# Duo attention and wave MLP on one core: V of the first batch in rows of six tokens, ordered by selecting matrices on TensorE; later V as one DMA a batch; filler products in the prologue; a new order of the steps on every engine

## The chip, the cores and the metric

One core of a Trainium2 chip. The metric is device microseconds of one execution (lower is better). All numbers with a point in time are microseconds from the start of the profiled span. The span in a profile is some 1.5 to 2 us shorter than the time. Engines: TensorE (PE in the profile, PEld its weight loads), VectorE (DVE), ScalarE (ACT), GpSimd (POOL), SyncE (SP). A run is called slow when it is over 1.5% above the fastest run of the same kernel; the others are called fast.

## The reference

Causal attention for 8 heads (three "retrieval" heads see everything before them, five "streaming" heads see 4 sink tokens and a window of 64), then an MLP that mixes tokens with a complex wave. B = 4, H = 8, S = 768, D = 64, d_model = 512.

```python
scores = q @ k.T / 8                       # per batch and head, 768 x 768
a = softmax(where(mask, scores, -1e9))
x = (a @ v) as [batch, 768, 512]
theta = x @ w_theta
zr, zi = x * cos(theta), x * sin(theta)
y = w_tok_r @ zr + w_tok_i @ zi            # over tokens
u = x + y
out = u + maximum(u @ w_ch, 0)
```

## The kernel before

The kernel describes its work as steps (engine, duration, what a step needs, which buffer it takes) and a small planner in the file orders them: list scheduling by the longest way to the end, plus a list `TILT` of corrections that was found by a search. The planner only fixes the order on each engine; on the chip each engine executes its own list in order and waits where something is missing.

```python
LATENCY = {"PE": (230, 0), "ACT": (190, 60), "DVE": (120, 60), ..., "DMA": (2000, 0), "DMAH": (2000, 0)}
rank[n] = longest way to the end + 100 * TILT[n]      # the highest rank that is ready goes first
...
def load_v(b, n, after=None):                # one pair of heads, rows of 64 f32 = 256 B
    src = v[b].rearrange("h (j p) d -> p h j d", p=128)
    ...
    for x, h in enumerate(PAIRS[n]):
        nc.sync.dma_start(out=t[:, x], in_=src[:, h])
def cast_v(b, n):                            # f32 -> bf16, DVE or GpSimd
    copy(vt[:, h0:h1 + 1:2, :, :D], state["v", b, n])
...
def v_steps(b):
    for n in range(4):
        if b == 0:
            issue = add("DVE", 200, lambda n=n: load_v(0, n, kT[n // 2]), [kept["k", 0, n // 2]], take="st_v")
            land = add("DMAH", 2000, None, [issue])
        else:
            issue = add("SP", 700, lambda b=b, n=n: load_v(b, n), [cast[b - 1, n], xk[b - 1, 5]], take="st_v")
            land = add("DMAH", 2000, None, [issue])
        cast[b, n] = add({"DVE": 570, "POOL": 830}, 0, lambda b=b, n=n: cast_v(b, n), [land] + old, give=[issue], port=True)
```

For each batch: 96 transposes of q and k, half-array scores (products that use half of the array's rows, some also half of its columns), exponentials on ACT, sink scores, value products (128x65), theta (24 products of 128x512), sines on ACT (another table than the exponential), z products on DVE, then 18 groups of four mix products and the channel products. Batch b+1's attention overlaps batch b's MLP. The value products need V with tokens on partitions; q, k (but for the first heads of batch 0) and the weights come by GpSimd's casting DMA.

The softmax here doesn't subtract the row's maximum and nothing guards it: scores larger than these inputs give would overflow.

## Time and profile before

| | before |
|---|---|
| time, median of the first 3 runs | 204.3 us (204.25 to 204.82) |
| span of the profiled run, mean granted clock | 201.1 us, 0.969 |
| TensorE, DVE, ACT busy | 88%, 64%, 52% |
| V of batch 0 landed | 23.45 |
| first theta product, last theta product | 34.38, 42.2 |
| TensorE idle before 50.63 | 3.96 us |

How to read it: TensorE is the busiest engine and from 60 us on it is nearly always busy, so the end is set by how much of TensorE's work is done by then. I use one derived number for that: *useful work by time t*, an estimate worked out from the traces. It counts the weight loads recorded until t (there is one for each product) and multiplies each by what a product of its shape takes at full clock in these traces (0.216 us for 512 columns, 31 ns for a value product, 56 or 28 ns for a transpose, 36 ns for a score, 56 ns for one of the few sink scores). Selecting and filling products are left out. The profile lines of the kernel before stand in the prediction.

Read the granted clock with care in the prologue. In the kernel before the column reads 1.00 until 25, while the starts of its products lie at half pace. The pace decides.

### The profile page before, as it was taken

The page shows a single profiled execution, that of the slowest core. Times are in us where ns is not written, and L with a number is a line of the kernel's source. Part 1 is how long each engine was busy: PE and PEld are TensorE (multiplying, and loading weights), DVE is VectorE, ACT ScalarE, POOL GpSimd, SP SyncE. Part 2 cuts the span into 40 slices and gives each one's busy share as a digit, 9 for nine tenths or more (in the row PEclk, how much of TensorE's full clock was granted, in tenths as well). Part 3 has the DMA queues.
Part 4 walks back from the last instruction along what each step waited for, and adds up shares of the span by engine and source line. Part 5 has one row for each costly group of instructions (what it writes and reads, how often), then busy time and mean ns, then how long its engine had stood idle before and what let it go on. Part 6 is the DMA issues. An engine that isn't in the chain of part 4 may idle for free.

```text
span 201.1 us, 4814 instructions
## 1 busy us (share of the span) xinstructions
PE 178.0 (88%) x1961; PEld 99.1 (49%) x1988; DVE 128.2 (64%) x229; ACT 104.6 (52%) x129; POOL 67.8 (34%) x141
## 2 busy tenths in 40 slices
PE   0689697992899998999899999999999999999981
PEld 0446496551444665645454565644434665444430
DVE  7336975892853785459965573698814776972461
ACT  2688814699167433388777605689774217700010
POOL 8987773542832360012284501024811100000000
PEclk9999969998599999999999999999999999999997
DMA  5998999999925199899149997579363564124512
GB/s 169 175 225 180 167 218 196 193 207 206 178 32 111 26 143 207 79 259 209 52 68 178 203 198 158 55 165 248 76 152 88 152 130 82 60 47 123 165 52 104
DMA packets 60652, 28.82 MB, mean 143 GB/s; under 512 B 44888, under 2 KB 57560, under 8 KB 60632
## 3 DMA queue, kind: packets, MB, share of 16 engines
q1 hardware_dynamic: 49816, 19.23, 45.7%
q0 software_dynamic: 10816, 9.31, 30.8%
q8 instruction: 15, 0.25, 0.5%
q14 instruction: 5, 0.04, 0.1%
HBM read 25.71 MB, written 6.29 MB: 159 GB/s over the span
## 4 chain that ended last, share of the span: by engine, by line
PE 71%; DMA 15%; ACT 5%; DVE 5%; issue 2%; SPq 0%; DVEq 0%; ACTq 0%
PE bank L555 28%; DMA st_v<-in_v_dram 10%; PE bank L578 9%; PE pair L419 9%; PE pair L532 8%; PE pair L506 8%; PE bank L353 6%; DMA xT<-x 3%; DMA uT<-u 3%; PE bank L598 2%; DVE zi L291 1%; ACT P_st L435 1%; PE bank L568 1%; ACT P L438 1%; DVE P_st L629 1%
## 5 line engine op out<-in xcount | busy, mean ns | idle before, releaser
L555 PE MATMUL bank<-zi,wtokTi 128*128 128x512 bf16 x139 | 39.0, 391 | 0.6 <-issue 0.5
L555 PE MATMUL bank<-zr,wtokTr 128*128 128x512 bf16 x134 | 37.2, 380 | 0.7 <-issue 0.2
L295 POOL TENSOR_SCALAR_AFFINE_SELECT P<-P 128x256 bf16<-128x256 bf16 (+1 forms) x48 | 18.4, 403 | 37.5 <-ACT P L438 19.0
L419 PE MATMUL pair<-qT,kT 64*64 64x128 bf16 (+6 forms) x380 | 26.2, 258 | 4.0 <-ACT P L438 1.5
L559 DVE TENSOR_TENSOR u<-x,bank 128x512 bf16<-128x512 bf16 x24 | 16.4, 687 | 15.9 <-PE bank L555 15.9
L438 ACT ACTIVATE P<-pair 128x1024 bf16<-128x1024 f32 (+2 forms) x24 | 21.5, 918 | 7.9 <-PE pair L419 7.8
L578 PE MATMUL bank<-w_ch_sb,uT 128*128 128x512 bf16 x89 | 23.3, 380 | 1.2 <-ACT uT L288 0.7
L532 PE MATMUL pair<-w_theta_sb,xT 128*128 128x512 bf16 x91 | 22.8, 379 | 1.1 <-DMA xT<-x 0.6
L419 PEld LDWEIGHTS <-kT 64*64 64x64 bf16 (+1 forms) x380 | 12.8, 109 | 20.4 <-issue 16.5
L555 PEld LDWEIGHTS <-wtokTi 128*128 128x128 bf16 x144 | 13.6, 100 | 17.0 <-issue 2.8
L582 DVE SCALAR_TENSOR_TENSOR ot<-bank,u 128x512 f32<-128x512 f32 x24 | 16.6, 690 | 8.2 <-PE bank L578 7.0
L291 DVE TENSOR_TENSOR zr<-x,ct 128x512 bf16<-128x512 bf16 x24 | 17.5, 760 | 3.4 <-ACT ct L537 3.0
L555 PEld LDWEIGHTS <-wtokTr 128*128 128x128 bf16 x144 | 12.4, 98 | 13.7 <-issue 1.3
L537 ACT ACTIVATE ct<-pair,half_pi 128x1024 f32<-128x1024 f32 x12 | 13.4, 1116 | 10.3 <-PE pair L532 7.1
L291 DVE TENSOR_TENSOR zi<-x,st 128x512 bf16<-128x512 bf16 x24 | 17.7, 758 | 0.0
L288 ACT COPY uT<-bank 128x512 bf16<-128x512 bf16 x5 | 2.9, 586 | 27.5 <-PE bank L568 27.5
L435 ACT ACTIVATE P_st<-pair 128x512 bf16<-128x512 f32 (+1 forms) x16 | 12.8, 812 | 8.5 <-PE pair L419 8.5
L513 DVE TENSOR_TENSOR x<-pair,r 128x512 bf16<-128x512 f32 x24 | 16.6, 692 | 0.8
L455 DVE TENSOR_TENSOR P_st<-P_st,m_stream 128x512 bf16<-128x512 bf16 (+2 forms) x24 | 12.0, 507 | 6.3 <-ACT P_st L435 5.2
L506 PE MATMUL pair<-vx,P_st 128*128 128x65 bf16 x120 | 15.5, 198 | 0.0
L506 PE MATMUL pair<-vt,P_st 128*128 128x65 bf16 x120 | 15.5, 198 | 0.0
L506 PE MATMUL pair<-vt,P 128*128 128x65 bf16 x252 | 14.9, 199 | 0.5 <-ACT P_st L435 0.5
(76 smaller groups left out, 270.0 us busy)
## 6 DMA issues: line engine op xcount, KB each, us to landing
st_v<-in_v_dram SPq DMA_DIRECT2D x32, 192.0 KB, 3.9
out_dram<-ot SPq DMA_DIRECT2D x24, 256.0 KB, 2.2
qb<-in_q_dram POOLq DMA_DIRECT2D x13, 192.0 KB, 6.0
kb<-in_k_dram POOLq DMA_DIRECT2D x13, 192.0 KB, 6.5
wtok<-in_moe_w_tok_r_dram POOLq DMA_DIRECT2D x3, 384.0 KB, 11.6
wtok<-in_moe_w_tok_i_dram POOLq DMA_DIRECT2D x3, 384.0 KB, 12.5
vx<-vt SPq DMA_DIRECT2D x3, 195.0 KB, 6.8
w_theta_sb<-in_moe_w_theta_dram POOLq DMA_DIRECT2D x1, 512.0 KB, 8.5
```

The source lines that it names most:

```text
L291: {"DVE": nc.vector, "POOL": nc.gpsimd}[state["step"].eng].tensor_tensor(o, a, b, ALU.mult)
L295: nc.gpsimd.affine_select(out=t, in_=t, compare_op=ALU.is_ge, fill=0.0, base=base, pattern=pattern, channel_multiplier=cm)
L419: nc.tensor.matmul(ps[half, yy, c:c + w], l, r, start=True, stop=True, skip_group_check=True)
L435: nc.scalar.activation(stream_out(banks[0][1], 2, q0, w), ps[:, :, :w].rearrange("p s (c x) -> p s c x", x=64), AF.Exp, scale=scale)
L438: nc.scalar.activation(P.rearrange("p (y c) -> p y c", y=2), ps[:, :, :w0], AF.Exp, scale=scale)
L506: nc.tensor.matmul(o, l, r, start=(m == 0), stop=True, skip_group_check=True)
L513: nc.vector.tensor_tensor(dst, av[:, :, :, :D], r.unsqueeze(3).to_broadcast([128, 2, 4, D]), ALU.mult)
L532: nc.tensor.matmul(ps[:, y], state["xT", b][:, kk, (i + y) * 128:(i + y + 1) * 128], w_theta_sb[:, kk], start=(kk == 0), stop=(kk == KD - 1))
L555: nc.tensor.matmul(py, wtokT[n][:, s, t * 128:(t + 1) * 128], z[:, s], start=(g == 0 and m == 0), stop=(g == 2 and m == 3))
L559: nc.vector.tensor_tensor(u, state["x", b][:, t], state.pop(("py", b, t)), ALU.add)
L578: nc.tensor.matmul(pc, uT[:, kk], w_ch_sb[:, kk], start=(kk == 0), stop=(kk == KD - 1))
L582: nc.vector.scalar_tensor_tensor(ot, state.pop(("pc", b, t)), 0.0, state.pop(("u", b, t)), ALU.max, ALU.add)
```

## The change

Intent: get V of batch 0 early and with large rows, so that the value products can start sooner; save DMA issues by loading the V of later batches in one piece; and keep TensorE's clock up in the prologue with small products.

- Batch 0: V comes by one casting DMA whose partition p holds tokens 6p to 6p+5 (1536 B rows). The order that the value products need is made on TensorE: six groups of six products with a 0/1 matrix `pick`, then ACT or DVE copies the sums to `vt`.
- Batches 1 to 3: one DMA for the whole V, four casts after it.
- 240 products `ident x ident` of 128 columns that the planner puts wherever TensorE would otherwise wait.
- The planner's model got a cold clock, contention between the two kinds of queues and a limit of DMAs in flight, the weight loads are no longer chained, and the list `TILT` was searched anew. So the order on every engine is another one.

```diff
+    def load_v0():
+        state["v0"] = t = v_room[:, 4:]...bitcast(BF16)...
+        nc.gpsimd.dma_start(out=t, in_=v[0].rearrange("h (p j) d -> p h (j d)", p=128))
+    def pick_v0(i):
+        pv = state["pv", i] = mine()
+        for j in range(NB):
+            c = 128 * i - j + NB - 1
+            nc.tensor.matmul(pv, pick[:, c:c + 128], state["v0"][:, :, j * D:(j + 1) * D], start=(j == 0), stop=(j == NB - 1))
+    def keep_v0(i):
+        copy(vt[:, :, i, :D], state.pop(("pv", i)).rearrange("p (h d) -> p h d", h=H))
...
-    def load_v(b, n, after=None):
...
-        for x, h in enumerate(PAIRS[n]):
-            nc.sync.dma_start(out=t[:, x], in_=src[:, h])
+    def load_v(b):
+        nc.sync.dma_start(out=v_room.rearrange("p h j d -> p (h j) d"), in_=v[b].rearrange("h (j p) d -> p (h j) d", p=128))
...
+    for n in range(240):
+        idle.append(add("PE", 56, lambda n=n: keep_busy(n), idle[-1:], ..., bias=-10 ** 9))
...
-    hold = [cast[0, 2]]
-    issue = add("POOL", 780, lambda: ...w_theta..., hold)
+    issue = add("POOL", 780, lambda: ...w_theta...)
...
 TILT = [ ... another list ... ]
(the rest of the planner's new model is cut)
```

## The prediction

> **What bounds the kernel now.** I read, in this order: the busy shares, the chain of waits that ended last, the busy times in stretches, TensorE's instructions in order of time, and the V tile's own view. The numbers in front are microseconds from the span's start.
>
> The busy shares first.
>
> ```profile
> PE 178.0 (88%) x1961; PEld 99.1 (49%) x1988; DVE 128.2 (64%) x229; ACT 104.6 (52%) x129; POOL 67.8 (34%) x141
> ```
>
> TensorE is the bound by share. Next: where do the missing 12% lie? The stretches say (columns: stretch, length, then busy time and count of TensorE, weight loads, DVE, ACT, POOL; granted clock, DMA share, GB/s):
>
> ```profile
> 15.00:20.00 5.00, 4.69 (x60) 3.10 (x58) 3.13 (x7) 4.24 (x7) 3.82 (x12) 1.00 0.92 184
> 20.00:25.00 5.00, 3.21 (x84) 2.48 (x80) 4.78 (x12) 4.50 (x7) 3.86 (x9) 1.00 0.96 163
> 25.00:30.00 5.00, 4.92 (x99) 4.61 (x96) 3.91 (x8) 0.65 (x2) 3.85 (x6) 0.66 1.18 218
> 45.00:50.00 5.00, 1.67 (x28) 0.94 (x25) 1.34 (x3) 4.83 (x6) 1.36 (x2) 0.89 1.21 211
> 50.00:60.00 10.00, 9.15 (x82) 4.50 (x86) 7.27 (x13) 3.56 (x6) 5.97 (x10) 0.72 0.57 105
> 60.00:70.00 10.00, 9.89 (x113) 5.34 (x107) 5.75 (x12) 5.66 (x8) 2.77 (x7) 1.00 0.33 67
> ```
>
> From 60 on TensorE is full (9.89 of 10), and stays at 98% or so. So only the first 56 us can be shortened by this change, and DMA is saturated there (share 0.92 to 1.21). The chain of waits shows what holds that stretch:
>
> ```profile
> 29.92 19.14 DMA st_v<-in_v_dram
> 49.06 0.03 issue
> ...
> 49.63 0.96 DVE kT L288
> ...
> 50.63 1.44 PE bank L598 x12
> ```
>
> The last V load of batch 1 takes 19.14 us from issue to landing; DVE waits in order behind its cast, and TensorE behind DVE (4.0 us idle). Then the instructions in order of time, for their pace:
>
> ```profile
> 9.71 0.85 PE L353 MATMUL bank<-ident,kb 128*64 128x128 bf16 x12
> 10.35 0.85 PE L353 MATMUL bank<-ident,qb 128*64 128x128 bf16 x12
> ...
> 25.16 0.25 PE L506 MATMUL pair<-vx,P_st 128*128 128x65 bf16 x1
> 25.21 0.25 PE L506 MATMUL pair<-vt,P_st 128*128 128x65 bf16 x1
> ...
> 29.25 0.19 PE L506 MATMUL pair<-vx,P_st 128*128 128x65 bf16 x1
> 29.28 0.19 PE L506 MATMUL pair<-vt,P_st 128*128 128x65 bf16 x1
> ...
> 38.15 0.53 PE L353 MATMUL bank<-ident,qb 128*64 128x128 bf16 x12
> 38.51 0.50 PE L353 MATMUL bank<-ident,kb 128*64 128x128 bf16 x12
> ```
>
> Look at starts, not durations. Twelve transposes take 0.64 us at 9.71 and 0.36 at 38.15; value products follow each other at 54 ns at 25 and at 30 ns at 29. TensorE runs at half speed from 5.2 to about 28.4, though the clock column says 1.00 until 25: the pace decides, the column has no record yet. After the 4 us gap it is slow again until about 56 (the 0.72 above).
>
> **What the Trainium skill says.** "TensorE: Matmul & The Clock Gate", What's actually happening: idle is 1.2 GHz, and about 3.4 us of sustained work gives 2.4 GHz. The trace agrees: dense value products from 24.5 to 28.4, 3.9 us, then twice the pace. The same page, Part 4: PE-mode transpose: transposes don't count as busy in the same way. The trace fits: TensorE was 4.69 of 5 us busy from 15 to 20, with half-array scores and transposes, and stayed slow. So the added full-array products should warm it. "DMA: Bandwidth & Descriptors", Specifications: at least 512 B per transfer for line rate, less is slow. V goes in 256 B pieces now, in 1536 B pieces (768 B after the cast) for batch 0 later. The trace gives 220 GB/s for V of batch 3 nearly alone (136 to 139), so 1.57 MB cost some 7 us of all engines; against it, q and k on the casting queue run at 145 to 184 GB/s of written bytes (5 to 8). Same page, SWDGE vs HWDGE vs iDMA: the cast in a DMA comes only from GpSimd; that is why batch 0's V moves to that queue.
>
> **The change part by part.**
> 1. V of batch 0: four f32 loads in 256 B rows and four DVE casts (0.56 us each) go; one casting load in 1536 B rows comes. It writes 0.79 MB, at some 165 GB/s 4.8 us instead of 7: 2 us of DMA less. It need no longer wait for K copies on DVE, so I expect it landed near 17 instead of 21.
> 2. Ordering V: 36 products of 128x512 by the selecting matrix. The theta products are the same shape, four in 0.86: 36 x 0.216 = 7.8 us of TensorE, plus six ACT copies of 128x512, 0.6 us each (ACT copies of uT take 0.586). In the changed order all 36 stand together in the middle of the scores, before sink scores and values: they are on the path.
> 3. 240 fillers of 128x128. Warm, 12 wtok transposes of that shape take 0.67 us from 33.48, 56 ns each: 13.4 us in all; the first 42 run at half speed, 2.4 us more. They stand where TensorE would wait, so mostly free; but they execute in order and also cost where it would not have waited.
> 4. Batch 1 to 3: V as one DMA of the same 256 B pieces. 24 issues of about 0.65 us on the queue's issuer become 3; the bytes cost the same, and no cast can start before all has landed.
> 5. A new order on every engine (read from the order of the built kernel's instructions, engine by engine): DVE now reaches V's casts only after eight of batch 0's twelve z products; more weight transposes come early.
>
> The sum, by equal work. Before reaches 56 having done: 96 transposes of q, k for batch 0 (8 x 0.34 = 2.7), scores 4, sinks 0.5, 148 value products (x 0.030 = 4.5), xT transposes 1.3, theta 24 x 0.216 = 5.2, batch 1's 96 transposes 2.7, 36 weight transposes 2.0, a few scores 0.6, 16 mix products 3.5: 27 us of warm work in 56.
>
> The changed order reaches its last filler having done 2.7 + 4 + 0.5 + 7.8 (selection) + 4.5 + 1.3 + 5.2 + two groups of batch 1 (0.7) + 48 weight transposes (2.7) = 29.4. With fillers 13.4 + 2.4 and a start at 1.4 (the identity is ready at 1.37) that is 46.6. To stand where before stood at 56 it lacks 27 + 7.8 - 29.4 = 5.4: 52.0. That is 4.0 us earlier if nothing else stalls.
>
> Against it I set stalls the fillers don't cover. GpSimd issues w_theta as number 38 of its queue, by its mask and memset durations near 21 (19.86 before). So DMA idles from 17 to 21, and what remains, 4.8 MB written by the casting queue and V's 1.57, takes 32 us at the 195 to 200 GB/s of before: until 53, no earlier than before. V, started after the selection near 27, competes and lands near 45 (before under contention: 1.57 MB at 4.4 us per 0.39 MB, 17.7 us); DVE gets there then. The last q, k of batch 1 land near 52 to 54, just when TensorE comes to them. I take 1.5 us for that, leaving 2.5. Fewer issues and a warm clock at 50 to 56 are partly in this already; for a better order in the full part (3.7 us of non-busy from 56 to 197) I give 0.8. Together 3.3: 204.3 - 3.3 = 201.0.
>
> **The rivals.**
> A. The fillers and selection eat the gain: the prologue was held by ACT and DMA, not by TensorE. For: ACT is busy 4.24 to 4.50 of 5 from 15 to 25, and gains 3.6 us of copies. Against: TensorE's half speed sits between ACT's steps in the chain. This makes 203 to 206.
> B. V of batch 1 lands later, as one piece behind the weights, and DVE stalls longer than before with all behind it. For: issue at 27 against 18, DMA full. Against: the bytes on the casting queue are spread and DVE's casts stand later. Landing at 50 instead of 45 would cost about 4: 204 or so.
> C. All of the hole at 46.7 to 50.6 and the slow stretch to 56 go, and loads come as they are needed: the full 4.0 plus 2 in the full part: 198.
>
> **The range.** The middle is 201.0; C and a milder A bound it: 197.8 to 204.4. Faster by 2% means under 200.2, slightly beyond the middle: 0.42. Within 2%: 0.53. Slower by 2% (over 208.4) needs B and A together: 0.05.
>
> **What would show it.** Right: value products of batch 0 at 30 ns from the first; 36 selecting products in about 8 us, ending near 27; no slow clock at 50 to 60; TensorE's idle before weight transposes (4.0) gone; last theta done near 43 to 46. V landing near 45 with DVE waiting under 2 us for it. Wrong: TensorE still slow among fillers; a wait of some us for weights before the values; a DVE wait of 4 us or more for V; waits for q, k loads at 46 to 54 of over 3 us; or idle time in the full part (TensorE under 97% busy from 60), where xT transposes may queue behind the single V load.

## The result

| | before | after |
|---|---|---|
| time, median of 4 runs of the same rounds | 204.28 us (203.52 to 204.82) | 207.42 us (206.90 to 207.69) |
| ratio, 95% interval | | 1.0154 (1.0115 to 1.0193) |
| span of the profiled run | 201.1 us | 205.2 us |

A ratio, here and below, compares the fast runs of one kernel with the fast runs of the kernel before from the same rounds. The us quoted beside it are medians of all runs, slow ones included, so the ratio of two medians is not quite the same. The change is 1.5% slower: within 2%, but above the range predicted (197.8 to 204.4).

The page of the changed kernel (its first part: busy time, share of the span, instructions):

```profile
PE 195.0 (95%) x2264; PEld 112.5 (55%) x2264; DVE 123.9 (60%) x226; ACT 110.8 (54%) x139; POOL 59.4 (29%) x135
```

TensorE is busier by 17 us and the kernel is slower: the fillers have 19.1 us of busy time by the profile's modelled ends, the selection 7.9 (some of it overlaps other instructions). A busy share that contains filler says nothing about useful work.

The busy times in stretches of the changed kernel (columns as in the prediction: stretch, length, then busy time and count of TensorE, weight loads, DVE, ACT, POOL; granted clock, DMA share, GB/s):

```profile
15.00:20.00 5.00, 5.00 (x105) 3.65 (x104) 3.25 (x5) 3.88 (x7) 4.14 (x17) 1.00 0.36 49
...
45.00:50.00 5.00, 5.00 (x59) 3.39 (x58) 4.44 (x7) 4.19 (x5) 0.82 (x1) 1.00 1.25 208
50.00:55.00 5.00, 3.51 (x79) 2.70 (x79) 4.96 (x10) 4.95 (x7) 0.35 (x1) 1.00 0.43 82
55.00:60.00 5.00, 4.94 (x41) 2.41 (x40) 3.79 (x7) 3.26 (x6) 0.58 (x2) 0.66 0.34 77
```

The hole of the kernel before at 45 to 50 is gone. In its place, from 50 to 55, DVE and ACT are completely full (4.96 and 4.95 of 5) and TensorE is not; then the clock falls to 0.66 while TensorE comes to the first mix products. Its instructions in order of time show the selection, the last fillers, and those mix products at half pace (eight products should take 1.73 us; they take 56.69 to 59.7):

```profile
21.11 7.93 PE L344 MATMUL bank<-v_room,pick 128*128 128x512 bf16 x36
...
49.92 0.84 PE L697 MATMUL bank<-ident 128*128 128x128 bf16 x12
...
56.69 1.89 PE L592 MATMUL bank<-zr,wtokTr 128*128 128x512 bf16 x4
58.37 1.37 PE L592 MATMUL bank<-zi,wtokTi 128*128 128x512 bf16 x4
```

The chain of what released what (start, duration, what), from the last theta to the first mix products of the changed kernel:

```profile
47.08 0.78 PE pair L569 x4
47.87 0.94 ACT st L576
...
48.90 1.11 ACT ct L574
...
50.73 1.03 ACT st L576
...
51.78 1.28 ACT L472
...
53.07 0.60 ACT P_st L472
...
54.25 1.05 ACT P_st L472
...
56.76 2.98 PE bank L592 x8
```

From 47.87 to 55.3 the chain lies on ACT: the sines of batch 0, the switch of the function table (51.78), then the first exponentials of batch 1, for whose buffers TensorE's scores wait. The Trainium skill, "ScalarE: Activation LUTs", What ACT_TABLE_LOAD costs, gives about 1283 ns for the load, and the trace has 1.28.

Useful work of TensorE, worked out as said above (us done by the time in the first column):

| by | before | after | before + 36 products | before, late cast | both | replanned |
|---|---|---|---|---|---|---|
| 30 | 10.0 | 6.0 | 6.1 | 10.2 | 6.1 | 8.8 |
| 45 | 22.1 | 17.4 | 16.3 | 20.4 | 16.9 | 20.8 |
| 50 | 23.5 | 20.9 | 20.8 | 24.2 | 21.1 | 24.6 |
| 60 | 30.0 | 25.7 | 29.1 | 33.2 | 29.5 | 33.3 |
| 70 | 38.3 | 34.7 | 38.1 | 42.1 | 38.3 | 42.7 |
| 100 | 65.4 | 61.7 | 65.0 | 67.7 | 66.3 | 68.8 |

The last four columns are experiments below. After is 4.3 us behind before at 60 and 3.7 at 100: all of the loss is made before 60, in two portions. Until 45 it is 4.7 behind, with the selection done in that time; between 45 and 60, where before stands in its hole and does only 7.9 us, after does no more (8.3) although no hole is there.

### The profile page after: what moved, and what is told of

Read it like the earlier page. It is cut to its first block, busy times and chain, and to the rows that moved or that the text cites. A ratio compares the mean times of both kernels' runs of the same rounds, so it can differ in the third digit from the quotient of the medians.

```text
span 205.2 us, 5357 instructions
## 1 busy us (share of the span) xinstructions
PE 195.0 (95%) x2264; PEld 112.5 (55%) x2264; DVE 123.9 (60%) x226; ACT 110.8 (54%) x139; POOL 59.4 (29%) x135
## 4 chain that ended last, share of the span: by engine, by line
PE 82%; DMA 5%; ACT 5%; DVE 4%; issue 2%; POOL 1%; DVEq 0%
PE bank L592 29%; PE bank L615 10%; PE pair L569 9%; PE pair L456 9%; PE pair L543 7%; PE bank L697 6%; PE bank L390 5%; DMA kb<-in_k_dram 5%; PE bank L344 4%; PE bank L635 1%; ACT ct L574 1%; ACT st L576 1%; DVE P_st L669 1%; ACT P_st L472 1%; PE pair L519 1%
## 5 line engine op out<-in xcount | busy, mean ns | idle before, releaser
L592 PE MATMUL bank<-zr,wtokTr 128*128 128x512 bf16 x144 | 39.6, 387 | 0.3 <-DVE zr L321 0.3
L325 POOL TENSOR_SCALAR_AFFINE_SELECT P<-P 128x256 bf16<-128x256 bf16 (+1 forms) x48 | 16.5, 366 | 49.9 <-ACT P L475 43.8
L615 PE MATMUL bank<-w_ch_sb,uT 128*128 128x512 bf16 x96 | 24.7, 380 | 0.7 <-ACT uT L318 0.7
L456 PE MATMUL pair<-qT,kT 64*64 64x128 bf16 (+6 forms) x380 | 23.1, 238 | 0.6 <-ACT kT L318 0.2
L697 PE MATMUL bank<-ident 128*128 128x128 bf16 x240 | 19.1, 231 | 1.4 <-POOL ident L644 1.4
L456 PEld LDWEIGHTS <-kT 64*64 64x64 bf16 (+1 forms) x380 | 11.7, 102 | 14.6 <-issue 9.9
L321 DVE TENSOR_TENSOR zr<-x,ct 128x512 bf16<-128x512 bf16 x24 | 16.5, 705 | 4.1 <-ACT ct L574 3.9
L550 DVE TENSOR_TENSOR x<-pair,r 128x512 bf16<-128x512 f32 x24 | 16.6, 691 | 0.8
L697 PEld LDWEIGHTS <-ident 128*128 128x128 bf16 x240 | 15.2, 104 | 3.2 <-POOL ident L644 1.4
L472 ACT ACTIVATE P_st<-pair 128x1024 bf16<-128x1024 f32 (+1 forms) x16 | 12.8, 810 | 6.6 <-PE pair L456 6.4
L321 DVE TENSOR_TENSOR zi<-x,st 128x512 bf16<-128x512 bf16 x24 | 15.9, 682 | 0.0
L318 ACT COPY uT<-bank 128x512 bf16<-128x512 bf16 x4 | 2.3, 586 | 23.5 <-PE bank L605 23.5
## 6 DMA issues: line engine op xcount, KB each, us to landing
v_room<-in_v_dram POOLq DMA_DIRECT2D x1, 768.0 KB, 12.1
```

Source lines behind the costliest of these rows:

```text
L321: {"DVE": nc.vector, "POOL": nc.gpsimd}[state["step"].eng].tensor_tensor(o, a, b, ALU.mult)
L325: nc.gpsimd.affine_select(out=t, in_=t, compare_op=ALU.is_ge, fill=0.0, base=base, pattern=pattern, channel_multiplier=cm)
L456: nc.tensor.matmul(ps[half, yy, c:c + w], l, r, start=True, stop=True, skip_group_check=True)
L550: nc.vector.tensor_tensor(dst, av[:, :, :, :D], r.unsqueeze(3).to_broadcast([128, 2, 4, D]), ALU.mult)
L592: nc.tensor.matmul(py, wtokT[n][:, s, t * 128:(t + 1) * 128], z[:, s], start=(g == 0 and m == 0), stop=(g == 2 and m == 3))
L615: nc.tensor.matmul(pc, uT[:, kk], w_ch_sb[:, kk], start=(kk == 0), stop=(kk == KD - 1))
```

## The experiments

All ratios are to the kernel before. Three theories stood at the start: **S**, the selection's 8 us on the path cost the time; **F**, the fillers or the clock of the prologue; **P**, the new order of the steps between 45 and 60. The runs went 3 or 5 rounds.

### The prologue: fillers and half clock

The changed kernel without its 240 fillers:

```diff
     def keep_busy(n):
         if n == 0:
             state["idle"] = mine()
-        nc.tensor.matmul(state["idle"][:, :128], ident, ident, start=True, stop=True, skip_group_check=True)
```

> The changed kernel without its 240 fillers, order otherwise the same. Theory F (fillers in order cost time where TensorE had no wait): 13 us of TensorE fewer, 203 to 205.5. Theory K (fillers keep the clock and pay): TensorE slow until the selection, 208.5 to 212. Neither: 206.5 to 208.

Measured: 207.88 us, ratio 1.0229 (1.0143 to 1.0315). And the kernel before with fillers (40 at the start, 8 ahead of each score group of batch 0):

```diff
         def multiply():
             cell["ps"] = ps = mine()
+            if b == 0:
+                for _ in range(8):
+                    nc.tensor.matmul(ps[:, 0, :128], ident, ident, start=True, stop=True, skip_group_check=True)
... (the 40 at the start are cut)
```

> The kernel before with 152 fillers only: 40 at the start and 8 ahead of each of batch 0's 14 groups of scores. Value products of batch 0 then follow at 30 ns instead of 54. If TensorE's half speed in the first 28 us cost time: 202.3 or less. If it was hidden behind ACT and the loads: 203.5 to 205.

Measured: 204.69 us, ratio 1.0042 (0.9941 to 1.0142), with the value products at full pace from the first (starts 30 ns apart, against 54 in the kernel before):

```profile
25.79 0.20 PE L509 MATMUL pair<-vx,P_st 128*128 128x65 bf16 x1
25.82 0.19 PE L509 MATMUL pair<-vt,P_st 128*128 128x65 bf16 x1
```

So fillers neither pay nor cost, within the intervals: half speed in the first 28 us was hidden behind other work. Behind which, ACT's or the DMA's, no run tests. F falls, and with it the hope that the fillers bring something.

### The selection: less of it, and the same load on the kernel before

The changed kernel with one product in place of six for each block (wrong result):

```diff
-        for j in range(NB):
+        for j in range(1):
... (start and stop of the one product are set to match)
```

> The changed kernel with 6 of the 36 selecting products (one per output block instead of six; result wrong on purpose), nothing else moved. Theory S (the selection lies on TensorE's path and is what the change pays for): 30 products fewer, 6.5 us of TensorE; the time falls by 5 to 6.5 us, to about 201 to 202.5. Theory P (the pile-up of ACT, DVE and a slow clock at 47 to 59 us, made by the new order, sets the time): the gain is absorbed there, time within 1.5 us of 207.4.

Measured: 206.39 us, ratio 1.0146 (1.0071 to 1.0222). Nearly nothing comes back. TensorE's instructions in order of time show why (in brackets the idle time before, and what ended it):

```profile
28.34 0.84 PE L635 MATMUL bank<-ident,wtok 128*128 128x128 bf16 x12 [2.96 <-DMA wtok<-in_moe_w_tok_i_dram]
```

A transpose of token weights stands ahead of the values in the new order, and their load lands at 28.3: a new wait takes the place of the work removed. Theta starts at 40.85 instead of 41.40. So the opposite run: the kernel before with 36 dummy products of the same shape at the same place (result correct):

```diff
         ps = state["sink_ps"] = mine()
+        if "sel" not in state:
+            state["sel"] = 1
+            for _ in range(36):
+                nc.tensor.matmul(ps[:, 0], ident, m_stream[:, :512], start=True, stop=True, skip_group_check=True)
```

> The kernel before, V loaded as it was, with only TensorE's cost of the selection added: 36 dummy products of 128x512 ahead of the sink scores of batch 0 (about 8 of them at half speed, so 9 to 10 us), which also warm the clock for the values. Theory S (selection ahead of the values delays values, theta and the sines, and what is left of the old 4 us hole cannot give that back): theta starts near 40 to 41 instead of 34.4, time 207 to 209. Theory P (the new order alone makes the loss; a delay of the values is swallowed by the V hole at 46.7 to 50.6): within 1.5 us of 204.3.

Measured: 202.75 us, ratio 0.9997 (0.9924 to 1.007). Its instructions in order of time, around the dummy products (one of the 36 has no record in the trace) and at the first theta:

```profile
23.47 9.63 PE L483 MATMUL pair<-m_stream,ident 128*128 128x512 bf16 x35
...
41.31 2.20 PE L536 MATMUL pair<-w_theta_sb,xT 128*128 128x512 bf16 x7
```

And the stretch of this run in which the kernel before had its hole:

```profile
45.00:50.00 5.00, 4.84 (x74) 2.84 (x75) 4.54 (x8) 3.47 (x5) 0.24 (x1) 1.00 1.20 212
```

Theta starts at 41.31 instead of 34.38, as late as in the changed kernel (41.40), and it costs nothing: TensorE is 4.84 busy at 45 to 50 where it had stood still (1.67). S in its simple form falls. But note what this run really shows: the products were free *in a kernel that had a hole behind them*.

### Other ways to bring V, and earlier loads

V of batch 0 straight into its place by the casting DMA, in rows of 64 elements, no selection:

```diff
-        nc.gpsimd.dma_start(out=t, in_=v[0].rearrange("h (p j) d -> p h (j d)", p=128))
+        nc.gpsimd.dma_start(out=vt[:, :, :, :D], in_=v[0].rearrange("h (j p) d -> p h j d", p=128))
```

> The changed kernel with V of batch 0 cast by the GpSimd queue straight into its place in 256 B rows; no selecting products, no copies of them on ACT; all else in the same order; result right. Theory S: falls by 6 to 8 us, to 199.5 to 201.5, if the small rows land before 29 us. Theory P: within 1.5 us of 207.4. If the small rows on the casting queue are slow (over 15 us), V lands after 29 and the values wait: no gain, for a new reason, seen as a wait for that DMA.

Measured: 221.22 us, ratio 1.0872. The DMA issues of this run (KB, us from issue to landing):

```profile
vt<-in_v_dram POOLq DMA_DIRECT2D x1, 768.0 KB, 23.4
```

In the changed kernel the same bytes in rows of six tokens take 12.1 us. Rows of 256 B read and 128 B written are twice as slow here (a factor of 1.9). The run is unclean as a test of the selection, since a GpSimd memset of `vt` and everything behind it waited as well.

Loads earlier: w_theta and the first token weights are issued some 7 us sooner than in the changed kernel.

```diff
... (the lists first_weights and qk_issues, filled where the loads are added, are cut)
+    early = [s for s in order if s in first_weights]
+    order = [s for s in order if s not in first_weights]
+    at = min(order.index(s) for s in qk_issues)
+    order[at:at] = early
```

> The changed kernel with w_theta and the first two weight loads issued 7 us earlier, into the time when DMA was idle (share 0.36 from 15 to 20 us); selection kept; result right. Theory S: the selection still gates, within 1.5 us of 207.4. If loads gate the middle (batch 1's q, k and V earlier by some us), 204 to 206.

Measured: 208.48 us, ratio 1.0254 (1.0187 to 1.0322). q and k of batch 1 land at 34 to 46 instead of 40 to 49, and nothing is gained: the order behind them stays, so earlier data wait. The same with V of batch 0 as one f32 load on the sync queue and ACT copies that cast, without selection:

```diff
-        nc.gpsimd.dma_start(out=t, in_=v[0].rearrange("h (p j) d -> p h (j d)", p=128))   (and the 36 products)
+        copy(vt[:, :, i, :D], v_room[:, :, i])                                            (load_v(0) on the sync queue)
```

> As the former, and V of batch 0 by one f32 load on the sync queue with the six ACT copies cast from it; no selecting products; result right. Both gates gone in a correct kernel. Theory S+W: 201.5 to 204. Theory P: 206 or more.

Measured: 207.85 us, ratio 1.0226 (1.0157 to 1.0295). This run does not test the selection either: the expectation took both waits for gone, but ahead of the values TensorE now waits 4.20 us for a load of k, and theta starts at 41.23, against 41.40 in the changed kernel.

```profile
27.07 0.85 PE L390 MATMUL bank<-ident,kb 128*64 128x128 bf16 x12 [4.20 <-DMA kb<-in_k_dram]
```

Then the changed kernel with six selecting products and the wait that took their place away too (four weight transposes read K instead of the late weights; wrong):

```diff
-            nc.tensor.transpose(pt[...], state["wtok", n, t][:, s * 128:(s + 1) * 128], ident)
+            src = state["k", 0][:, 4, :128] if t < 2 else state["wtok", n, t][:, s * 128:(s + 1) * 128]
+            nc.tensor.transpose(pt[...], src, ident)
```

> The changed kernel with 6 of 36 selecting products and with the first four weight transposes reading K, long there, in place of the weights they would wait for (wrong on purpose): both gates ahead of the values taken away. Theory S with a second gate W (weights placed ahead of the values, 3 us of wait once the selection is gone): values start near 28, 202 to 203.5. Theory P: as with 6 products alone, 206 to 207.5.

Measured: 205.77 us, ratio 1.0142 (1.0072 to 1.0212). Theta starts at 36.95, 4.5 us sooner. Of a lead of 3.2 us of useful work at 40 (16.1 against 12.9), 1.6 is left at 60 (27.3 against 25.7), and the ratio is not clear of the changed kernel's 1.0154. The busy times in two stretches:

```profile
45.00:50.00 5.00, 3.18 (x85) 2.70 (x85) 5.00 (x10) 4.95 (x7) 0.12 (x2) 1.00 1.26 206
50.00:55.00 5.00, 4.78 (x38) 2.38 (x34) 4.08 (x8) 3.89 (x6) 2.43 (x3) 0.55 0.77 164
```

The picture is the changed kernel's own, 4.5 us earlier: DVE and ACT full, TensorE idle, then half clock.

### Is it the order? Both kernels searched again

The list `TILT` of the changed kernel, searched again for ten minutes by random changes against the kernel's own planner; its makespan (a model's number) falls from 196.5 to 190.0. All steps stay.

```diff
-TILT = [-34, 231, 104, 532, ...]
+TILT = [another list]
```

> The changed kernel with the same steps (selection, fillers, single V loads all kept) in another order: only the list of priorities that the kernel's own planner uses was searched again, from the changed kernel's list, until the planner's makespan fell from 196.5 to 190.0. By the plan TensorE then has 39.7 us of useful steps done at 60 instead of 36.5, and the loads of q and k of batch 1 stand before w_ch and the second token weights. Theory P (the parts are harmless, the order chosen for 45 to 60 us costs): 200 to 203, with most of the gain before 60, and the first mix products well before 56. Rival R (selection, fillers or the single V load cost by themselves, whatever the order): 205 to 208.

Measured: 205.35 us, ratio 1.0133 (1.0048 to 1.0217), less than P expected. The mean of the fast runs is 1.7 us under the changed kernel's (205.66 against 207.36), but from other rounds, in which the kernel before was 1.0 us faster too (203.21 against 204.22); by the ratios (1.0133 against 1.0154) nothing clear is gained. The control, the same search for the kernel before:

> Control: the kernel before, all steps kept, its list of priorities searched again in the same way and as long (its planner's makespan falls from 184.7 to 181.1, by a model that knows neither the half clock nor the contention of the two kinds of queues). If search depth alone moves the time as much as in the changed kernel, this gains 2 to 4 us too: 200 to 202. If the changed kernel's order was the poor one: within 1.5 us of before, 202 to 205.5.

Measured: 201.86 us, ratio 0.9891 (0.977 to 1.0012). The search gives 2.3 us (200.93 against 203.21; the interval just reaches no gain) to the kernel before, so the distance between the two does not shrink. P as the whole cause falls. A third version without selection, its weights issued first, V of batch 0 as f32 load, planned from zero:

> The changed kernel without selection: V of batch 0 comes as one f32 load in 256 B rows on the sync queue and is cast by ACT or DVE, w_theta, the first token weights and q, k of batch 1 are issued first, w_ch and the other token weights behind them; the list of priorities searched for it from zero (planner's makespan 190.7). TensorE has 7.8 us less to do before the values. Theory P: 199 to 203, since the order was made for it. If TensorE's selection counted (theory S, fallen once): clearly under the reordered changed kernel, by 2 us or more; if not: within 1.5 us of it.

Measured: 207.04 us, ratio 1.0199 (1.0118 to 1.028), a miss. V of batch 0 was issued at 6.53 and landed at 26.0, 19.5 us later, where the planner had assumed 8. Weights and loads of k were issued from 9 to 14 in the meantime; that they took the bandwidth is likely, not shown.

### The hole and the selection, one by one and together

The run with dummy products left a question that can be asked directly: what is the hole worth alone, and what do the products cost once it is gone? In the kernel before, DVE stands at 45.5 before the cast of batch 1's last V pair, with z products behind it that are ready. One step is moved:

```diff
     order = plan.order({"PE": 0, "ACT": 2100, "DVE": 2500, "POOL": 7500, "SP": 750})
+    late = [s for s in order if s.n in (229, 230)]        # DVE's cast of V pair 3, batch 1, and the copy that needs it
+    order = [s for s in order if s.n not in (229, 230)]
+    at = [s.n for s in order].index(197) + 1              # behind batch 0's last z product
+    order[at:at] = late
```

> The kernel before with one step moved: DVE's cast of the last V pair of batch 1 (and the copy of V that needs it) stands behind the z products of batch 0 instead of ahead of them, so DVE does not stop at 45.5 for the load that lands at 49.1. All loads and all other steps stay. If the hole is what the path waits for (the prediction's own reading): TensorE's idle of 4.0 us before 50.6 shrinks to under 1 us, and the time falls by 2 to 3.5 us, 200.5 to 202. If the hole is slack, filled by other waits (weights that land at 46.5 to 48.9, ACT): within 1 us of before.

Measured: 200.54 us, ratio 0.9798 (0.9709 to 0.9886); only three of its six runs were fast (197.06, 198.29, 199.97), the profile is of a slow one, and the record's verdict at 2% is unclear. DVE's instructions around the cast, in the kernel before and then with the cast moved:

```profile
49.15 0.56 DVE L288 CAST vt<-st_v 128x768 bf16<-128x768 f32 x1 [3.66 <-DMA st_v<-in_v_dram]
```

```profile
51.67 0.68 DVE L291 TENSOR_TENSOR zr<-x,ct 128x512 bf16<-128x512 bf16 x1
52.27 0.55 DVE L288 CAST vt<-st_v 128x768 bf16<-128x768 f32 x1
```

And the busy times in the stretch of the former hole:

```profile
45.00:50.00 5.00, 4.72 (x70) 3.04 (x66) 4.03 (x8) 4.85 (x7) 2.94 (x6) 1.00 1.20 211
```

The cast now waits for nothing, TensorE is busy 4.72 instead of 1.67, and the slow clock behind the hole is gone too (1.00 from 50 to 60, against 0.72). The Trainium skill, "PSUM — Partial Sum Buffer", Engine vs sequencer instructions, says that the queues of ScalarE, VectorE and GpSimd are strict FIFO; this is what it means in practice. Now the same with the 36 products:

> The same with 36 products of 128x512 ahead of batch 0's sink scores, as in the run with dummy products on the kernel before (which cost nothing: ratio 0.9997). If those were free only because of the hole: with the hole gone they cost 2 to 4 us against the kernel with the late cast alone, 203 to 205. If they are free in any case: within 1 us of the kernel with the late cast.

Measured: 202.71 us, ratio 1.003 (0.9971 to 1.0089), in the same 5 rounds as the last one. The four corners:

| | without products | with 36 products |
|---|---|---|
| with the hole | 1 (by definition) | 0.9997 |
| without the hole | 0.9798 | 1.0030 |

With the hole, the products cost nothing; without it, they cost 2.4% (203.15 against 198.44 by the means, 4.7 us). The sizes rest on the three fast runs of the late cast: over all runs of these two kernels, slow ones included, the means are 200.50 and 203.15, 1.3% apart. The direction has a second witness: the late cast with the single V load (below, 0.9862 by six fast runs) also lies clear of 1.003. So in the kernel before, the hole and the products fill the same time. The changed kernel removed the hole *and* added the selection. That this is what it pays is argued, not shown: its own runs with fewer selecting products (1.0146, 1.0142) gave back nothing clear.

### What holds 45 to 60 in the changed kernel

Less work for ACT and DVE: q, k copies of batch 1 cut to 64 of 768 columns and its V casts to one block of six (wrong):

```diff
+        if b == 1:
+            copy(dst[:, :64], pt[:, :64])
+            return
... (the V casts are cut short in the same way)
```

> The changed kernel with the q, k copies of batch 1 cut to 64 of 768 columns and its V casts cut to one of six blocks: some 7 us less work on ACT and DVE together between 40 and 63, wrong result on purpose, everything else in place. If ACT and DVE bound that stretch (theory P2): TensorE's useful work between 45 and 60 rises from 8.3 us to 11 or more and the time falls to 203 to 205. If TensorE's own order or its half clock bound it: under 1 us of gain, 206.4 to 207.5.

Measured: 205.20 us, ratio 1.0129 (1.0071 to 1.0188). In the profiled run, useful work between 45 and 60 rises from 8.3 to 10.5 us, short of the 11 expected; the lead is 2.3 us at 80 and gone at 90, where this (slow) run waits for k of batch 2, by TensorE's instructions in order of time:

```profile
85.06 0.85 PE L393 MATMUL bank<-ident,kb 128*64 128x128 bf16 x12 [2.44 <-DMA kb<-in_k_dram]
```

So ACT and DVE do hold part of that stretch, but how much it is worth at the end this run does not settle. Then the same work in another order: DVE makes the last three z products ahead of the V casts, and TensorE takes the first mix products earlier:

```diff
+    by[561].slot, by[435].slot = 3, 0
+    for who, behind in ((406, 408), (328, 406), (431, 432), (561, 431), (409, 426), (407, 409), (512, 407),
+                        (464, 512), (463, 464), (462, 463), (461, 462), (465, 461), (562, 501)):
+        put(who, behind)
```

> The changed kernel with the same work in another order in one place: DVE makes the last three z products (which the first mix needs) ahead of the V casts of batch 1, and TensorE takes the first eight mix products at about 52.5 and 55 instead of 56.7 and 58.4; result correct. If the order of DVE and the half clock behind it made the loss (theory P): clock 1.0 in 55 to 60, useful work at 60 up by 1.5 to 3 us, 204.5 to 206. If ACT and DVE together are the bound (P2): the work is only shuffled, within 1 us of the changed kernel, 206.4 to 208.

Measured: 207.64 us, ratio 1.0242 (1.0185 to 1.03). The busy times in the stretch that was slow, then a line of TensorE's instructions in order of time:

```profile
55.00:60.00 5.00, 4.05 (x47) 2.21 (x49) 3.77 (x8) 4.93 (x8) 2.55 (x3) 1.00 0.15 33
```

```profile
65.18 0.45 PE L519 MATMUL pair<-qT,kS 128*32 128x512 bf16 x5 [1.54 <-POOL kS L379]
```

The clock stays at 1.00, the mix products run at 53.2 and 55.7 instead of 56.7 and 58.4, 1.1 us is won at 60, and 5 us later TensorE waits 1.54 us for sink keys on GpSimd. So the half clock at 55 to 60 is not what sets the end: without it the time stays, and another wait takes the gain.

### The single V load, and an order planned with measured landings

> The kernel before with the late cast (ratio 0.9798 to before), and V of batches 1 to 3 as one load a batch, issued where the last of the four pair loads was issued; casts unchanged in place. If the single load costs in the changed kernel (every cast waits for the whole 1.57 MB, GpSimd's casts at 40.0 and 45.6 first): 1 to 3 us over the late cast alone, 201.5 to 203.5. If it is neutral: within 0.8 us of it, 199.7 to 201.3.

```diff
-            for x, h in enumerate(PAIRS[n]): nc.sync.dma_start(out=t[:, x], in_=src[:, h])   (batches 1 to 3)
+            nc.sync.dma_start(out=v_room.rearrange("p h j d -> p (h j) d"), in_=v[b].rearrange("h (j p) d -> p (h j) d", p=128))
```

Measured: 200.74 us, ratio 0.9862 (0.9823 to 0.99), against 0.9798 with four pair loads; the intervals overlap, so 0.6% is suggested, not shown. In its profiled run (slow) TensorE stands still again at 40 to 45, busy 1.39 of 5, as all casts wait for the whole load.

Last, the kernel before with its planner told what the trace shows, and the list searched again:

```diff
-    theta_w = add("DMA", 3300, None, [issue])
+    theta_w = add("DMA", 9600, None, [issue])
-                land = add("DMAH", 2000, None, [issue])
+                land = add("DMAH", 4700 if b == 1 else 2000, None, [issue])
                 ns = s.on[e]
+                if e == "PE" and t < 26000:
+                    ns *= 1.9
```

> The kernel before, all steps kept, its planner told three things that the trace showed: w_theta lands 6.3 us later than it assumed, each V pair of batch 1 takes 4.7 us instead of 2.0, TensorE runs at about half pace before 26 us; then the list of priorities searched again. If what was wrong with the order was its assumed landings: at or under the late cast alone, 197 to 200.5. If a search gains no more than the blind one (201.86, ratio 0.9891): 200.5 to 202.5.

Measured: 198.14 us, ratio 0.9729 (0.9685 to 0.9773), the best of all versions and correct. The list was searched four times for twelve minutes, and the order with the shortest makespan was run. The busy times in the stretch of the hole:

```profile
45.00:50.00 5.00, 4.84 (x53) 2.51 (x54) 5.00 (x8) 4.97 (x7) 0.53 (x2) 1.00 1.18 204
```

The blind search of the same kernel gave 0.9891 (0.977 to 1.0012). But this search was also longer (four times twelve minutes against ten), so how much of the difference comes from the measured landings is not shown.

## Why the prediction was wrong

By its own steps:

1. *Only the first 56 us can be shortened, DMA is saturated there, TensorE is full later.* Right: what after is behind at 60 (4.3) it is behind at 100 (3.7).
2. *The last V load of batch 1 holds DVE, DVE holds TensorE.* Right, and shown: moving that one cast is worth 2.0% by its fast runs. But the remedy lay in DVE's order, not in the loads.
3. *V of batch 0 near 17.* It landed at 16.6. *Selection 7.8 us, ending near 27.* It took 7.9, from 21.1 to 29.0. *Last theta done near 43 to 46.* Wrong: 48.8.
4. *Fillers cost nothing much and warm TensorE.* They do both, and the warmth pays nothing that the runs can show. Rival A of the prediction is right in so far as TensorE's pace did not hold the prologue; that the fillers eat the gain is not. Its 203 to 206 was the nearest, and still too low.
5. **The step that failed** is the sum by equal work: "To stand where before stood at 56 it lacks 27 + 7.8 - 29.4 = 5.4: 52.0." It treats everything as TensorE work that follows without gaps. The last filler ended at 50.8 instead of 46.6, 4.2 us later (in that time TensorE's list of waits has only 1.2 us after its start; what makes up the rest is not worked out). From there it took until about 60.7 before the useful work reached what the kernel before had at 56 (26.0 us): 9.9 us instead of 5.4. Together that is 8.7 us; the allowance for stalls was 1.5. In place of the 5.4 the trace shows the chain on ACT from 47.87 to 55.3, with TensorE's short steps between ACT's, and the half clock behind it.
6. The sum also has no term for what the hole and the selection share. It counts the selection's 7.8 us as work that fills TensorE, in a kernel where the hole is gone. The four corners show, for the kernel before, that the two share the same time: late cast and 36 products together come to 1.003, not below 1.
7. *No slow clock at 50 to 60.* Wrong: 0.66 at 55 to 60. The prediction itself quoted, for the prologue, that transposes do not count as busy in the same way, and did not apply it to 50 to 55, where TensorE had only transposes, half-array scores and ten fillers. That this is the reason is not shown.
8. *V of batch 1: DVE waits under 2 us.* Right: DVE came to the casts at 51.31 and waited for nothing. GpSimd, off the path, waited 5.79 us for it with its own cast, until 47.02. *q and k of batch 1 at 52 to 54.* Wrong (40 to 49), without effect, as the run with earlier loads showed.

What stays open: the changed kernel (1.0154) is still about 1.2% slower than the kernel before with late cast and 36 products (1.003). A new search (1.0133) or less work on ACT and DVE (1.0129) may each give back a part, and the single V load may cost some 0.6%, but none of these is clear of its interval. No run isolates the rest, so the cause of the whole loss stays open.

## What to carry to other kernels

Price work that you add against the slack of the kernel as it will be, not as it is: a hole that the change removes cannot also hide the work that the change adds, and three experiments (without the hole, with the work, both) say so before the change is written. Where an engine stands in order before a load and ready work lies behind, move that one step first; here it gave 2.0%, by three fast runs. And give a planner the landings and paces of a trace before searching its order: a search gained 1.1% with assumed landings, and a longer one 2.7% with measured ones.

## What the Trainium skill lacked or had wrong

- "DMA: Bandwidth & Descriptors", Why small descriptors are slow: it works out 27% of overhead for a descriptor of 256 B. The casting load of V in such rows (128 B as written) took 23.4 us from issue to landing, against 12.1 us for the same 768 KB in rows of 1536 B (768 B as written): nearly twice, with the issue at 4.5 in both. The page does not say that its 27% is all of the loss, and the runs don't separate the reading from the writing side.
- "ScalarE: Activation LUTs", What ACT_TABLE_LOAD costs: 1283 ns fits (1.28 us), but the drain of about 1380 ns that the page adds for each switch is not seen here: the last sine ended at 51.76 and the first exponential began at 53.07, 1.31 us in all.
- "TensorE: Matmul & The Clock Gate": for transposes it says that they don't count as busy in the same way; I found nothing on half-array products. Here TensorE was 3.51 of 5 us busy from 50 to 55 with transposes, half-array scores and ten small full-array products (1.49 us were idle), and the clock was 0.66 in the next 5 us.
